# Low parts of the first layer's weights by TensorE and ACT instead of POOL, in a kernel of attention, a Fourier mix and a two-layer network

## The chip, the cores and the metric

The kernel runs on one core of one Trainium2 chip. The metric is the device time of one execution in microseconds (us). Five engines work side by side, each through its own list of instructions in order: TensorE (PE; its weight loads are shown as PEld), VectorE (DVE), ACT, POOL and SP, which here only issues transfers. Matrix products go to PSUM, in banks of 128 x 512 float32 numbers; everything else lies in SBUF.

## The reference

```python
def _attn_ref(q, k, v):                        # 8 batches, 8 heads, 576 positions, 64 wide
    scores = scale * np.matmul(q, k.transpose(0, 1, 3, 2))
    scores = np.where(block_i >= block_j, scores, -1e9)      # blocks of 64
    attn = np.exp(scores - np.max(scores, axis=-1, keepdims=True))
    attn = attn / (np.sum(attn, axis=-1, keepdims=True) + 1e-09)
    return np.matmul(attn, v)

def _moe_ref(x, w_ch1, w_ch2):                 # x: 8 x 576 x 512, weights 512 x 2048 and 2048 x 512
    X = np.fft.fft(np.fft.fft(x, axis=1), axis=2)
    u = x + np.real(X)
    un = (u - mean(u)) / np.sqrt(var(u) + 1e-06)
    return u + np.maximum(un @ w_ch1, 0.0) @ w_ch2
```

`x` is the output of the attention with the heads side by side. The weights are float64, all else is float32.

## The kernel before, in words

To keep the accuracy of float32 with float16 products, the kernel splits each operand in a high part, rounded to float16, and a low part, the rest, also float16. A product is then three products: high by high, high by low, low by high. This is done for the weights (`W`, with index 0 the high and 1 the low part), for the normalized rows (`uh`, `ul`), the hidden layer (`gh`, `gl`, later kept in tiles that are named `zc`, `zs` and `fs` after earlier users), the probabilities (`ph`, `pl`) and V (`VH`, `VL`).

The work goes batch by batch. For each head there are four products for the row maxima (tile `M`), four for the scores, and the values (`av`, 45 products). When the eight heads of a batch are done, a Fourier transform by products with constant tables follows (`dft`): rows are gathered (`U`, `X`, `u`), folded on VectorE (`tmp`, `fs`), multiplied in two stages (`fs` to `zc` and `zs`, these to `bs`, `dif` and `add`), and POOL adds the results to `u`. Then 256 rows at a time are normalized (`st`, `ag`, `un`), transposed (`uh`, `ul`) and given as a "feed" to the two layers: `h` is the first layer's result, `acc` the second's. A feed has 192 first-layer and 96 second-layer products and fills gaps that the heads leave.

The weights are prepared during the first batch and a half. A load brings two tiles of 128 x 512 (the last four loads one each) as 64-bit words. "Unpacking" (`weight_single`) makes float32 numbers of their bits with one `TENSOR_SCALAR` and two `SCALAR_TENSOR_TENSOR` on VectorE (rows `W<-W` or, for the last four, `W<-u`), then ACT sums their squares (`left`). When a layer's sixteen tiles are unpacked, `weight_scale` makes a power of two out of the sum (`wst`), and `weight_parts` splits each tile: for the second layer by ACT and VectorE, for the first by ACT (high part, and a scaled copy in a scratch tile named `p32`, shown as `p`) and POOL (copy less high part). Raw tile `i` lies where parts `i + 2` will lie, so the parts follow each other in order.

The order of all instructions is set by a planner at build time. Each piece of work is a `Step` with a cost on TensorE, a chain of costs on other engines (D VectorE, A ACT, G POOL, X VectorE and the shared queue K, p the two scratch tiles, B a PSUM bank coming free), the steps that it comes after, and keys that must be done. The planner books queues with these costs and takes from several lanes what is ready; steps of the second batch's heads wait until the first layer's weights are done (`("w", 15)`). The lists of the engines are fixed by it, so a changed cost moves other work too. Almost every instruction is recorded by a helper, so in the profile PE's line is 217 and the other engines' is 195.

Of the kernel before, what the change touches and what calls it, by code (L numbers as in the profile page):

```python
# [9 lines left out]
F32 = mybir.dt.float32  # L10
F32R = mybir.dt.float32r
F16 = mybir.dt.float16
I32 = mybir.dt.int32
AF = mybir.ActivationFunctionType
ALU = mybir.AluOpType
# [4 lines left out]
B, H, S, D = 8, 8, 576, 64  # L20
DM = H * D
FF = 4 * DM
P = 128
NF = FF // P
# [177 lines left out]
def tile_attn_fourier_ffn(  # L202
# [5 lines left out]
    work = pool("work")  # L208
# [4 lines left out]
    def ps_tile():  # L213
        return ps[current].tile([P, 512], F32, name=current)

    def mm(*args, **kw):
        return tc.keep_in_program_order(nc.tensor.matmul(*args, **kw))  # L217
# [4 lines left out]
    vector, scalar, gpsimd, sync = (Ordered(tc, x) for x in (nc.vector, nc.scalar, nc.gpsimd, nc.sync))  # L222
# [4 lines left out]
    ident = ident_r.bitcast(F32)  # L227
# [24 lines left out]
    X1, X0, QA, QB = [], [], [], []  # L252
# [23 lines left out]
    for at in range(0, NCOS, P):  # L276
        w = min(P, NCOS - at)
        vector.tensor_scalar(ZT[:, at:at + w], ones[:, 0:w], 0.0, None, op0=ALU.mult)

    W = const.tile([P, 2 * NF + 2, 2, DM], F16, name="W")  # L280
# [14 lines left out]
    def may(step):  # L295
        return all(x in done for x in step.after) and all(x in done for x in step.need)

    def ready(step):
        r = max((done[x] for x in step.after), default=0.0)
        return max(r, min(rings[x][0] for x in lent)) if step.bank else r  # L300
# [780 lines left out]
    wst = work.tile([P, 8], F32, name="wst")  # L1081
# [28 lines left out]
    def weight_single(x):  # L1110
        i, n, at = LANDS[x]
        r = raw(x).rearrange("p (n x) -> p x n", x=2)
        t = W[:, i + 2:i + 2 + n].rearrange("p i x n -> p (i x n)").bitcast(I32)
        vector.tensor_scalar(t, r[:, 1], 3, 0x3FFFFFFF, op0=ALU.logical_shift_left, op1=ALU.bitwise_and)
        yield
        vector.scalar_tensor_tensor(t, r[:, 0], 29, t, op0=ALU.logical_shift_right, op1=ALU.bitwise_or)
        yield
        vector.scalar_tensor_tensor(t, r[:, 1], -(1 << 30), t, op0=ALU.bitwise_and, op1=ALU.bitwise_or)
        yield
        scalar.activation(wjunk[:, 0:DM * n], t.bitcast(F32), AF.Square, accum_out=wsum[:, i:i + 1])  # L1120
        if n == 2:
            gpsimd.memset(wsum[:, i + 1:i + 2], 0.0)
        yield

    def weight_sum(w):
        vector.tensor_reduce(wst[:, 4 * w:4 * w + 1], wsum[:, NF * w:NF * (w + 1)], axis=AX.X, op=ALU.add)
        yield

    def weight_scale(w):

        n2, sc, inv = (wst[:, 4 * w + i:4 * w + i + 1] for i in range(3))
        t = ps_tile()
        mm(t[:, 0:1], ones, n2, start=True, stop=True)
        yield
        vector.tensor_copy(n2, t[:, 0:1])
        e = (10, 14)[w]
        x = work.tile([P, 1], I32, name="pw", bufs=2)
        vector.tensor_scalar(x, n2.bitcast(I32), 0x7F000000, 1, op0=ALU.bitwise_and, op1=ALU.logical_shift_right)
        vector.tensor_scalar(sc.bitcast(I32), x, -1, (190 + e) << 23, op0=ALU.mult, op1=ALU.add)
        vector.tensor_scalar(inv.bitcast(I32), x, (64 - e) << 23, None, op0=ALU.add)  # L1140
        if w == 1:
            vector.tensor_tensor(inv_w, wst[:, 2:3], wst[:, 6:7], op=ALU.mult)
        yield

    def weight_parts(i):
        t = W[:, i + 2].rearrange("p x n -> p (x n)").bitcast(F32)
        w = i // NF
        sc = wst[:, 4 * w + 1:4 * w + 2]
        scalar.activation(W[:, i, 0], t, AF.Copy, scale=sc)
        yield  # L1150
        if w == 0:
            scaled = work.tile([P, 512], F32, name="p32", bufs=2)
            scalar.activation(scaled, t, AF.Copy, scale=sc)
            yield
            gpsimd.tensor_tensor(W[:, i, 1], scaled, W[:, i, 0], op=ALU.subtract)
            yield
            return
        vector.scalar_tensor_tensor(W[:, i, 1], t, sc, W[:, i, 0], op0=ALU.mult, op1=ALU.subtract)
        yield

# [10 lines left out]
    def weight_lane(w):  # L1171

        for x, (i, n, at) in enumerate(LANDS):
            if i // NF == w:
                yield Step(
                    lambda: weight_single(x), 0.0, (f"D{0.19 + 0.53 * n}", f"D{0.19 + 0.51 * n}", f"D{0.19 + 0.51 * n}", f"A{0.38 + 0.43 * n}"),
                    (("WL", x),) + ((("WS", x - 1),) if x else ()) + ((("scale", 0), ('V', 7, 4)) if w else ()), ("WS", x),
                )
        if w == 1:
            yield Step(lambda: None, 0.0, (), (), "w32")  # L1180
        yield Step(lambda: weight_sum(w), 0.0, ("D0.16",), tuple(("WS", x) for x, y in enumerate(LANDS) if y[0] // NF == w), ("sum", w))
        yield Step(lambda: weight_scale(w), 0.1, ("B", "D0.45"), (("sum", w),), ("scale", w), True)
        for j in range(NF):
            yield Step(
                lambda: weight_parts(NF * w + j), 0.0, ("A0.73", "X0.75") if w else ("A0.73", "p1", "A0.72", "G1.2", "p"), (("scale", w),) + ((("w", NF * w + j - 2),) if NF * w + j > 1 else ()), ("w", NF * w + j),
            )

    def store(b, c):
# [25 lines left out]
    lanes = [table_lane(), head_lane(), prepare_lane(), pair_lane(), copy_lane(), v_lane(), max_lane(), score_lane(), value_lane(), transform_lane()]  # L1214
    heads = [next(x) for x in lanes]
    weights, filler = [load_lane(), *(weight_lane(w) for w in range(2))], None
    sides = [next(x) for x in weights]
    while True:
# [23 lines left out]
        else:  # L1242
            w = None
# [5 lines left out]
        if soon:  # L1249
            i = min(soon, key=lambda i: heads[i].place)  # L1250
        elif feed and ready(filler) <= now or feed and not able:
            i = None
        elif able:
            i = min(able, key=lambda i: ready(heads[i]))
        elif any(sides):
            w = min((w for w, x in enumerate(sides) if x is not None and may(x)), key=lambda w: ready(sides[w]))
# [62 lines left out]
```

## Time and profile before

| | |
|---|---|
| runs (us) | 1246.78, 1252.19, 1253.78; median 1252.19 |
| profiled execution (us) | 1252.79, span 1251.0 |
| mean granted TensorE clock | 0.937 |
| busy: PE, PEld, DVE, ACT, POOL | 92%, 66%, 57%, 45%, 35% |

In the rows of the profile, "x3" counts the instructions of a row and `out<-in` names tiles. Rows by time give the start, the time from the first start to the last end of the row, the engine and the operation, and in brackets how long the engine was idle before and what ended that. Rows by stage give, for each stretch of time, its length, then the busy time of PE, PEld, DVE, ACT and POOL with counts, the granted TensorE clock, and the share and rate of the transfers. Rows by group give busy time and mean ns, then the idle time before them; rows by tile give the shortest, median and longest duration in ns and the first and last start.

### The profile page before, as it was taken

The numbers are of one execution on the slowest core, as the hardware profiler recorded it, in microseconds if no ns is written. First come the engines' busy times: TensorE is split into PE (matmuls) and PEld (weight loads), VectorE is DVE, ScalarE is ACT, GpSimd is POOL, SyncE is SP. The second block draws the span as 40 slices with busy tenths as digits, with TensorE's granted clock in tenths as the row PEclk, the third lists the DMA queues.
The fourth block names the chain that finished last, engine by engine and source line by source line (L and its number), as shares of the span: only waits on it lengthen the run. The fifth ranks groups of instructions, "written<-read, shape, count | busy, mean of one in ns | idle before, by whom it ended". The sixth has DMA issues, their size and how long they took to land.

```text
span 1251.0 us, 25235 instructions
## 1 busy us (share of the span) xinstructions
PE 1145.8 (92%) x10068; PEld 829.5 (66%) x10068; DVE 709.6 (57%) x1520; ACT 562.3 (45%) x1249; POOL 433.4 (35%) x522
## 2 busy tenths in 40 slices
PE   5773387999799999999999999999999999999998
PEld 4662374577577777776667767776777667766665
DVE  6878778776656664756647665576545324421211
ACT  5555656755464554644555445554542112111110
POOL 4654732433443633353343533335342200300000
PEclk9655776999799999999999999999999999999999
DMA  7684334361334232431335232422230110000000
GB/s 208 194 266 139 106 103 126 78 176 41 97 93 124 53 106 75 114 109 52 88 87 153 73 86 69 123 73 85 69 84 15 37 37 1 22 18 1 18 18 17
DMA packets 65099, 107.38 MB, mean 86 GB/s; under 512 B 9504, under 2 KB 35304, under 8 KB 64982
## 3 DMA queue, kind: packets, MB, share of 16 engines
q1 hardware_dynamic: 57606, 81.37, 23.5%
q10 hardware_dynamic: 4384, 16.78, 4.0%
q0 software_dynamic: 2992, 7.62, 2.2%
q8 instruction: 79, 1.29, 0.5%
q14 instruction: 38, 0.31, 0.1%
HBM read 58.54 MB, written 18.89 MB: 62 GB/s over the span
## 4 chain that ended last, share of the span: by engine, by line
PE 79%; DVE 10%; POOL 3%; DMA 3%; issue 2%; ACT 2%; SPq 0%; DVEq 0%; ACTq 0%; POOLq 0%
PE acc L217 30%; PE h L217 29%; PE ps L217 14%; PE av L217 6%; DVE W L195 3%; DVE M L195 2%; DMA lead<-mt 1%; PE ps L220 1%; POOL u L195 1%; DVE VL L195 1%; DVE rest L195 1%; DMA U<-xd,rows 1%; POOL pl L195 1%; SPq L195 0%; POOL ag L195 0%
## 5 line engine op out<-in xcount | busy, mean ns | idle before, releaser
L217 PE MATMUL h<-uh,W 128*128 128x256 f16 x2304 | 427.6, 273 | 2.0 <-DVE gl L195 1.2
L195 POOL TENSOR_TENSOR pl<-p,ph 128x288 f16<-128x288 f32 (+1 forms) x256 | 255.2, 1012 | 410.5 <-ACT p L195 395.2
L217 PEld LDWEIGHTS <-W 128*128 128x128 f16 x3456 | 332.1, 98 | 65.0 <-issue 3.7
L217 PE MATMUL acc<-W,gh 128*128 128x512 f16 x1104 | 330.4, 381 | 1.1 <-DVE W L195 1.0
L217 PE MATMUL h<-ul,W 128*128 128x256 f16 x1152 | 314.5, 273 | 0.3 <-issue 0.3
L195 ACT ACTIVATE gh<-h 128x512 f16<-128x512 f32 x138 | 82.4, 598 | 295.5 <-PE h L217 295.3
L217 PE MATMUL acc<-W,gl 128*128 128x512 f16 x552 | 209.6, 380 | 1.3 <-DVE gl L195 1.3
L195 DVE SCALAR_TENSOR_TENSOR gl<-h,gh 128x512 f16<-128x512 f32 x138 | 94.6, 688 | 204.2 <-ACT gh L195 204.1
L195 DVE TENSOR_REDUCE M<-ps 128x1 fp32r<-128x320 f32 (+3 forms) x293 | 132.1, 487 | 127.1 <-PE ps L217 126.7
L217 PE MATMUL ps<-lead 73*128 73x288 f16 (+13 forms) x694 | 165.4, 300 | 17.1 <-DMA lead<-in_c_masks_dram 7.0
L195 ACT ACTIVATE ph<-ps 128x288 f16<-128x288 f32 (+1 forms) x231 | 116.4, 506 | 98.7 <-PE ps L217 97.9
L217 PEld LDWEIGHTS <-gh 128*128 128x128 f16 x1104 | 102.5, 99 | 83.9 <-issue 3.8
L217 PEld LDWEIGHTS <-ph 128*128 128x128 f16 x1920 | 116.9, 105 | 23.1 <-issue 2.6
L217 PE MATMUL av<-VH,pl 128*128 128x65 f16 x960 | 119.0, 203 | 7.0 <-POOL pl L195 6.8
L217 PE MATMUL av<-VH,ph 128*128 128x65 f16 x960 | 120.2, 205 | 1.5 <-DVE zc L195 1.5
L217 PE MATMUL av<-VL,ph 128*128 128x64 f16 x960 | 119.4, 202 | 0.0
L195 ACT ACTIVATE p<-ps 128x288 f32<-128x288 f32 (+1 forms) x231 | 116.6, 507 | 2.7 <-POOL pl L195 2.7
L217 PE MATMUL ps<-rest 128*128 128x320 f16 (+3 forms) x344 | 97.6, 296 | 7.2 <-DVE M L195 6.2
L217 PEld LDWEIGHTS <-pl 128*128 128x128 f16 x960 | 95.7, 104 | 9.1 <-POOL pl L195 8.8
L217 PEld LDWEIGHTS <-gl 128*128 128x128 f16 x552 | 53.9, 98 | 70.1 <-DVE gl L195 3.3
L217 PEld LDWEIGHTS <-lead 73*128 73x128 f16 (+1 forms) x672 | 58.2, 101 | 62.6 <-issue 20.8
L217 PEld LDWEIGHTS <-rest 128*128 128x128 f16 x336 | 34.0, 101 | 21.8 <-issue 3.5
(186 smaller groups left out, 1427.0 us busy)
## 6 DMA issues: line engine op xcount, KB each, us to landing
raw<-in_qk_dram SPq DMA_DIRECT2D x28, 576.0 KB
W<-in_moe_w_ch_dram ACTq DMA_DIRECT2D x14, 1024.0 KB
rest<-lead SPq DMA_DIRECT2D x72, 144.0 KB
V<-in_v_dram SPq DMA_DIRECT2D x32, 320.0 KB
out_dram<-u SPq DMA_DIRECT2D x32, 256.0 KB
rest<-rest SPq DMA_DIRECT2D x56, 144.0 KB
xd<-x SPq DMA_DIRECT2D x30, 256.0 KB
u<-xd SPq DMA_DIRECT2D x8, 512.0 KB
```

The costliest lines, as they stand in the source:

```text
L195: x = f(*args, **kw)
L217: return tc.keep_in_program_order(nc.tensor.matmul(*args, **kw))
L220: return tc.keep_in_program_order(nc.tensor.transpose(*args, **kw))
```

## The change

The first layer's low parts are no longer made by POOL from a scaled copy. Two tiles are made once: `ident` times minus the scale in float32, and `ident` in float16; both lie in a tile named `x`, which also holds the attention's results on their way out. For each weight tile TensorE then computes, in one PSUM bank, the float32 product of the first with the unpacked tile plus the float16 product of the second with the high part. That is the high part less the scaled weight, and ACT writes it with the opposite sign as the low part. The high part becomes a step of its own (`weight_high`), and the steps have new costs: 1.2 on TensorE, 0.6 on ACT, nothing on POOL, and no scratch tile.

```diff
+    turns = []
+
+    def weight_high(i):
+        t = W[:, i + 2].rearrange("p x n -> p (x n)").bitcast(F32)
+        scalar.activation(W[:, i, 0], t, AF.Copy, scale=wst[:, 1:2])
+        yield
+
     def weight_parts(i):
...
+        if w == 0:
+            if i == 0:
+                both = work.tile([P, 10 * D], F32, name="x", bufs=1)
+                turns.extend((both[:, 0:P], both[:, P:P + P // 2].bitcast(F16)))
+                vector.tensor_scalar(turns[0], ident, sc, -1.0, op0=ALU.mult, op1=ALU.mult)
+                vector.tensor_copy(turns[1], ident)
+                yield
+            left = ps_tile()
+            mm(left, turns[0], t, start=True, stop=False)
+            mm(left, turns[1], W[:, i, 0], start=False, stop=True)
+            yield
+            scalar.activation(W[:, i, 1], left, AF.Copy, scale=-1.0)
+            yield
+            return
         scalar.activation(W[:, i, 0], t, AF.Copy, scale=sc)
         yield
-        if w == 0:
-            scaled = work.tile([P, 512], F32, name="p32", bufs=2)
-            scalar.activation(scaled, t, AF.Copy, scale=sc)
-            yield
-            gpsimd.tensor_tensor(W[:, i, 1], scaled, W[:, i, 0], op=ALU.subtract)
-            yield
-            return
...
+            if w == 0:
+                yield Step(
+                    lambda: weight_high(j), 0.0, ("A0.73",), (("scale", 0),) + ((("w", j - 2),) if j > 1 else ()), ("whigh", j),
+                )
+                yield Step(
+                    lambda: weight_parts(j), 1.2, (("D0.5",) if j == 0 else ()) + ("A0.6",), (("whigh", j),), ("w", j), True,
+                    need=(("V", 5, 4),),
+                )
+                continue
```

The planner's order changes from there to the end. On TensorE, in the first batch's Fourier transform, before (`dft` with `fs` and `uh` is the first stage):

```order
L217 MATMUL h<-ident,M_90 5x128
L217 MATMUL h<-dft,fs_1295 128x290 x3
L217 MATMUL h<-dft,fs_1307 128x290 x3
L217 MATMUL h<-dft,fs_1291 128x290
L217 MATMUL acc<-dft,fs_1295 128x290 x3
```

and after the change, where `W,x` is a product of a weight tile with one of the two new tiles:

```order
L217 MATMUL ps<-W,x 128x512
L217 MATMUL h<-dft,fs_1305 128x290 x3
L217 MATMUL h<-dft,fs_1319 128x290 x3
L217 MATMUL h<-dft,fs_1300 128x290
L217 MATMUL h<-W,x 128x512
L217 LDWEIGHTS x
L217 MATMUL h<-W,x 128x512
L217 MATMUL acc<-dft,fs_1305 128x290 x3
```

Six of the sixteen pairs of products stand ahead of the first stage, seven between the products of the two stages, and three behind them. On ACT, where the splitting begins, before (`lead`, `rest` and `VH` are the high parts of heads 8 and 9):

```order
L195 ACTIVATE W<-W,wst 128x512
L195 ACTIVATE p_1209<-W,wst 128x512
L195 ACTIVATE W<-W,wst 128x512
L195 ACTIVATE p_1215<-W,wst 128x512
L195 ACTIVATE lead_1155<-raw,vacc 128x576
L195 ACTIVATE rest_1156<-raw,vacc 128x576
L195 ACTIVATE VH_94<-V,vacc 128x10x64
```

and after (`W<-acc` and `W<-ps` are low parts out of PSUM):

```order
L195 ACTIVATE W<-W,wst 128x512 x2
L195 ACTIVATE W<-acc 128x512
L195 ACTIVATE lead_1155<-raw,vacc 128x576
L195 ACTIVATE rest_1156<-raw,vacc 128x576
L195 ACTIVATE VH_94<-V,vacc 128x10x64
L195 ACTIVATE W<-ps 128x512
```

The first low part, which waits for TensorE, stands ahead of head 8's high parts. On VectorE, in feed 1's first layer, before (`zc`, `zs` and `fs` are low parts of the hidden layer, the last of them `fs`; `W<-W` and `W<-u` are unpackings, `M_90` belongs to head 10):

```order
L195 SCALAR_TENSOR_TENSOR zc_1910<-h,zc_1910 128x512
L195 SCALAR_TENSOR_TENSOR zc_1922<-h,zc_1922 128x512
L195 TENSOR_SCALAR W<-W 128x1024
L195 SCALAR_TENSOR_TENSOR W<-W 128x1024 x2
L195 SCALAR_TENSOR_TENSOR zs_1957<-h,zs_1957 128x512
L195 TENSOR_REDUCE M_90<-ps 128x2
L195 TENSOR_REDUCE M_90<-ps 128x1 x3
L195 SCALAR_TENSOR_TENSOR zs_2024<-h,zs_2024 128x512
L195 SCALAR_TENSOR_TENSOR fs_2038<-h,fs_2038 128x512
L195 TENSOR_SCALAR W<-u 128x512
```

and after, a little earlier in it:

```order
L195 TENSOR_SCALAR W<-u 128x512
L195 SCALAR_TENSOR_TENSOR W<-u,W 128x512 x2
L195 TENSOR_REDUCE M_90<-ps 128x2
L195 TENSOR_REDUCE M_90<-ps 128x1
L195 TENSOR_SCALAR W<-u 128x512
L195 SCALAR_TENSOR_TENSOR W<-u,W 128x512
L195 TENSOR_REDUCE M_90<-ps 128x1
L195 SCALAR_TENSOR_TENSOR zc_1941<-h,zc_1941 128x512
```

Before, five unpackings are left when the second `ul` of feed 1 is made, and three of them come behind feed 1's first layer. Now four are left, and all four stand within it. The earlier ones have moved too: one more whole unpacking stands ahead of the first fold, and the one that stood right behind the last Fourier sum of the batch stands before that sum.

More of the change, by code (lines that the diff above doesn't have):

```diff
@@ L1183, in weight_lane @@
         for j in range(NF):
+            if w == 0:
[7 more added lines that the diff above has]
+                continue
             yield Step(
-                lambda: weight_parts(NF * w + j), 0.0, ("A0.73", "X0.75") if w else ("A0.73", "p1", "A0.72", "G1.2", "p"), (("scale", w),) + ((("w", NF * w + j - 2),) if NF * w + j > 1 else ()), ("w", NF * w + j),
+                lambda: weight_parts(NF * w + j), 0.0, ("A0.73", "X0.75"), (("scale", w), ("w", NF * w + j - 2)), ("w", NF * w + j),
             )
```

## The prediction

> **What bounds the kernel now.** I read the slices of the page first, then the busy time by stage, then the chain that ended last inside the stage of the change, then the engines' rows there.
>
> ```profile
> PE   5773387999799999999999999999999999999998
> PEclk9655776999799999999999999999999999999999
> ```
>
> From the eighth slice on (one is 31 us) TensorE is full and at its full clock, but for a dip at slice 11. What happens before that counts only by how much TensorE work it leaves undone. The same by stages:
>
> ```profile
> core 0: us, PE busy (x) PEld busy (x) DVE busy (x) ACT busy (x) POOL busy (x), PEclk, DMA share, GB/s
> 96.00:116.00 20.00, 2.42 (x9) 0.97 (x8) 17.77 (x28) 12.68 (x22) 11.84 (x13) 0.50 0.57 184
> 116.00:143.00 27.00, 16.04 (x83) 13.08 (x83) 19.08 (x29) 15.90 (x32) 15.09 (x18) 0.75 0.18 59
> 143.00:165.50 22.50, 10.12 (x75) 6.80 (x76) 21.84 (x34) 12.34 (x30) 14.08 (x20) 0.50 0.24 77
> 190.00:222.00 32.00, 22.63 (x165) 14.47 (x163) 27.67 (x63) 20.12 (x47) 8.08 (x9) 0.68 0.36 109
> 319.00:341.00 22.00, 14.60 (x115) 10.15 (x116) 15.36 (x36) 8.29 (x20) 10.76 (x17) 0.69 0.34 99
> ```
>
> "Loss" below means length less busy time times clock. From 96 to 165.5 us TensorE does 1.2 + 12.0 + 5.1 = 18 us of full-clock work in 69.5 us, a loss of 51. From 190 to 222 it loses 32 - 22.63 x 0.68 = 16.6 and from 319 to 341 it loses 11.9. So there are two places to win: the stage of the change (96 to 165.5), and 190 to 222, where the second layer's weights are late. There VectorE is the busy engine.
>
> In the stage of the change VectorE and POOL hold each other up:
>
> ```profile
> 98.56 0.68 DVE L195 TENSOR_SCALAR W<-W 128x1024 int32<-128x1024 int32 x1
> 100.46 0.85 DVE L195 SCALAR_TENSOR_TENSOR VL<-V,vacc,VH 128x640 f16<-128x640 f32 x1
> 110.86 0.68 DVE L195 TENSOR_TENSOR tmp<-X,U 33x512 f32<-33x512 f32 x1 [1.43 <-DMA U<-xd,rows]
> 113.09 0.42 DVE L195 TENSOR_TENSOR fs<-tmp,fs 32x257 fp32r<-32x257 f32 x1
> 114.42 2.95 DVE L195 TENSOR_TENSOR fs<-tmp,fs 128x257 fp32r<-128x257 f32 x1 [0.46 <-ACT p L195]
> 143.67 5.90 DVE L195 TENSOR_SCALAR W<-W 128x1024 int32<-128x1024 int32 x1
> 181.85 0.68 DVE L195 TENSOR_SCALAR W<-W 128x1024 int32<-128x1024 int32 x1
> 182.57 2.49 DVE L195 SCALAR_TENSOR_TENSOR W<-W 128x1024 int32<-128x1024 int32 x2
> 211.17 0.17 DVE L195 TENSOR_REDUCE wst<-ul 128x1 f32<-128x16 f32 x1 [0.92 <-ACT left L195]
> ```
>
> ```profile
> 114.80 2.27 POOL L195 TENSOR_TENSOR W<-p,W 128x512 f16<-128x512 f32 x2
> 142.89 1.15 POOL L195 TENSOR_TENSOR W<-p,W 128x512 f16<-128x512 f32 x1
> 146.77 2.25 POOL L195 TENSOR_TENSOR W<-p,W 128x512 f16<-128x512 f32 x2
> ```
>
> A VectorE instruction that meets POOL's subtractions lasts until these are over: 2.95 us from 114.42 while two run (a like one took 0.42), 5.90 from 143.67 (the same form took 0.68 at 181.85), until 149.57, with the last subtraction over at 149.02. Both lie on the chain that ended last, and some of the subtractions themselves too (start, us, what):
>
> ```profile
> 114.42 2.95 DVE fs L195
> ...
> 132.86 1.33 POOL W L195
> 134.28 2.02 POOL W L195
> ...
> 139.04 1.14 POOL W L195
> ...
> 143.75 5.84 DVE W L195
> ...
> 165.47 7.50 PE h L217 x51
> ```
>
> Until 110.86 the chain is the gather that VectorE waits for in that row; what POOL holds up ahead of it costs nothing.
>
> **What is removed.** Sixteen subtractions of 1.29 us leave POOL:
>
> ```profile
> L195 POOL TENSOR_TENSOR W<-p,W 128x512 f16<-128x512 f32 x16 | 20.5, 1291 | 13.4 <-ACT p L195 13.1
> ```
>
> POOL's 20.5 us have no worth of their own, only the stalls do, and what of them stands on the chain. At 114.42 it is 2.95 - 0.42 = 2.5 us. Three pieces of the chain are subtractions that stand ahead of the Fourier sums on POOL: 1.33 + 2.02 + 1.14 = 4.5. At 143.67 POOL's own additions on the Fourier sums run in any case, but without the 1.15 ahead of them and the 2.25 behind them the block ends 3.4 us sooner. Sum: 10.4 us off the chain.
>
> **What is added.** ACT reads sixteen low parts of 512 columns from PSUM, a form that takes 0.60, where it wrote sixteen scaled copies of that size: one for one, no charge. VectorE makes the two diagonals once: at most the 0.68 of the 1024 columns at 98.56 for each, rather 0.3, since they have 128. TensorE gets, for each tile, a float32 product of 512 columns and a float16 one. Its rows:
>
> ```profile
> L195 ACT ACTIVATE gh<-h 128x512 f16<-128x512 f32 x138 | 82.4, 598 | 295.5 <-PE h L217 295.3
> L220 PE MATMUL ps<-ident,un x64: 272/273/308, 447.2 to 860.6; 128*128 128x128 f32 x64
> L217 PE MATMUL h<-uh,W x256: 269/273/417, 165.5 to 307.6; 128*128 128x256 f16 x128
> L217 PE MATMUL acc<-W,gh x80: 376/379/393, 217.1 to 317.5; 128*128 128x512 f16 x80
> 213.84 1.92 PE L220 MATMUL ps<-ident,un 128*128 128x128 f32 x8
> ```
>
> A float32 instruction of 128 columns lasts as long as a float16 one of 256 (273), and four transposes are eight records: each float32 product is two passes at half the rate. From 256 to 512 float16 columns is 379 - 273 = 106 ns more, so 512 float32 columns are 2 x 4 x 106 = 0.85 us, the float16 product 0.21, together 1.07 us at full clock (at least 0.64, were it three float16 products). At half clock the eight records took 1.92, 0.24 per 128 columns and pass, so 8 x 0.24 + 0.43 = 2.35 us. I take 1.2 and 2.4 with weight loads. Sixteen are 19 us of TensorE work at full clock, which fits the loss of 51: no charge, unless a tile stands ahead of something on the chain. It does at two places, and the new order adds a third charge.
>
> First, ACT's order now has the first low part ahead of head 8's high parts (`lead`, `rest`) and VH, which were done early:
>
> ```profile
> 97.45 0.78 ACT L195 ACTIVATE lead<-raw,vacc 128x576 f16<-128x576 f32 x1 [0.33 <-DVE vacc L195]
> 99.17 0.82 ACT L195 ACTIVATE VH<-V,vacc 128x640 f16<-128x640 f32 x1
> ```
>
> The diagonals come about 99.2, the first tile ends at 102 (half clock), the low part at 102.6, and with two high parts and VH of some 0.7 to 0.8 each VH ends at 104.8, where VectorE had started on VL at 100.46. VectorE then still has VL, an unpacking, head 8's low parts and maxima (about 6 us unblocked), and one whole unpacking (0.68 + 2.49) that the order moved up to here. So the fold that started at 110.86 starts near 114: +3.1. Second, seven tiles stand between the Fourier stages. The clock, 0.50 in the row from 96 to 116, rises within the stages of before:
>
> ```profile
> 119.00:122.40 3.40, 3.40 (x13) 2.93 (x14) 3.27 (x8) 1.70 (x5) 0.00 (x0) 0.50 0.00 0
> 122.40:125.80 3.40, 3.24 (x17) 2.43 (x15) 2.58 (x6) 1.37 (x4) 0.00 (x0) 0.65 0.00 0
> ```
>
> After 3.4 us at work without a break it begins to rise (0.65 as the mean of the next 3.4 us, so about 5 us in all). So one or two tiles cost 2.4 and the rest 1.2; VectorE's unpackings, now 3.2 each, cover all but the first two: +3.5. The Trainium skill has this rule in "TensorE: Matmul & The Clock Gate", Part 1: about 3.4 us of sustained work lifts the gate, about as long an idle stretch drops it again. By it the tiles from 99 us on would themselves have lifted the clock, and the second charge would be 2.4 instead of 3.5; the rows above agree that work alone lifts it, after a little longer.
>
> Third, unpackings move ahead. The one at 143.67 now stands before the last Fourier sum. There it still waits for POOL's additions and then adds 0.68 + 2.49 = 3.2; behind the sum it no longer costs the rest of its 5.90 (2.5) and its two further passes (2.5): -1.8. The one of 181.85 takes the place ahead of the second `ul` that the one before it had, so its own time costs nothing; for its load, which is asked for later than that one's, and POOL's work beside it I take +1.5 (0 to 4). Together `ul`, on which feed 1 waits, moves by -10.4 + 3.1 + 3.5 - 1.8 + 1.5 = -4.1. Feed 1, at 165.47 before, starts some 5.8 earlier, for head 9's scores no longer stand ahead of it; these cost 1.3 at full clock later. So the first term is **-4.5** (bounds: +9 if all seven tiles cost 2.4 on the path, 16.8 instead of 3.5; -12 if none of the charges falls on it, 10.4 + 1.8).
>
> **The second term** is 190 to 222. The unpacking of 181.85 would end near 156, and the four last ones, and the sum at 211.17 that all second-layer weights wait for, follow in the order one by one within feed 1's first layer instead of behind it. TensorE then has second-layer products to fill the 16.6 us of loss. VectorE does the same work as before, so I take half of it: **-8.5** (bounds 0 and -16.6).
>
> Sum: -13 on a profiled time of 1252.8 (span 1251.0; the median of runs is 1252.2): **1240 us**. What hides TensorE's 19 us is idle time; what may be late next is head 15, which ends the dip at 319 to 341.
>
> **Rivals.** *All of the second loss comes back*: -4.5 - 16.6, 1232. For it: the order has second-layer products before head 10's end, where it had none. Against: VectorE was at 27.67 of 32 there. *Nothing reaches the end*: the lead of the first layers is spent waiting at 319 to 341, where TensorE hangs on the next batch's heads and not on weights; the 11.9 us lost there would grow by the 13 won, 1253. *Slower*: TensorE stays at half clock, because ACT and TensorE now wait for each other (a high part waits for the product two tiles earlier, in a buffer that both read), and each of the seven tiles puts 2.4 us between Fourier stages that follow one another directly. Then the first term is its upper bound, +9, and with none of the second term the time is 1262. It decides, with the second term, from 2.4 us per tile on the chain (7 x 2.4 is about 3.5 + 13), without it from 1.1 (3.5 + 4.5). Against it is the clock's rise at 122.4. *The change doesn't do what it says* is no rival: the order has no subtraction on POOL left.
>
> **Chances.** Forecast (1235 to 1246) 0.43; second loss wholly back (below 1235) 0.20; nothing reaches the end (1246 to 1258) 0.21; slower (above 1258) 0.16. A change of 0.5%, 6.3 us, is about what a measurement of this kernel can tell from none. So faster 0.63, same 0.21, slower 0.16. The range 1228 to 1260 leaves out the last part of both outer cases.
>
> **What would show it.** Right: the `fs` row at 0.4 instead of 2.95, no VectorE row of 5.9, feed 1 near 160, the sum of second-layer squares near 190 instead of 211, TensorE losing about 8 between there and 222. Wrong: the fold starts well after 114 (ACT behind the first tile costs more), the granted clock stays 0.50 past 125, tiles of over 2 us stand on the chain, or the dip after 319 grows.

## The result and the profile after

The changed kernel is faster: median 1235.82 us (1232.19 to 1236.84, four runs) against 1252.99 of the kernel before beside it, ratio 0.9866 with a 95% interval from 0.9825 to 0.9907. The profiled execution took 1235.12, span 1233.3, mean granted clock 0.959. A second set of six runs of the same kernel, told below, gave 0.9915 (0.9898 to 0.9933). So the gain is some 11 to 17 us, and the forecast of 13 lies between.

The stages that the prediction used, and 251 to 319, to which the dip moved:

```profile
96.00:116.00 20.00, 13.56 (x24) 4.94 (x25) 14.02 (x25) 11.09 (x21) 3.69 (x6) 0.67 0.66 219
116.00:143.00 27.00, 23.70 (x102) 15.02 (x102) 21.46 (x35) 19.38 (x40) 10.09 (x15) 0.88 0.16 48
143.00:165.50 22.50, 12.16 (x107) 8.70 (x107) 19.07 (x39) 13.64 (x31) 10.25 (x16) 0.70 0.48 152
190.00:222.00 32.00, 27.00 (x266) 16.21 (x267) 25.12 (x53) 25.66 (x57) 12.67 (x13) 1.00 0.42 109
251.00:319.00 68.00, 61.66 (x549) 44.16 (x548) 51.09 (x110) 35.96 (x83) 31.58 (x39) 0.92 0.37 106
319.00:341.00 22.00, 21.97 (x234) 17.07 (x233) 13.04 (x33) 12.07 (x29) 8.46 (x11) 1.00 0.21 53
```

From 190 to 222 TensorE loses 5.0 us (32 - 27.00 x 1.00) where it lost 16.6. The dip that lay at 319 to 341 lies ahead of 319 now and costs 68 - 61.66 x 0.92 = 11.3, about the 11.9 of before: it moved with the work and did not grow. In the stage of the change (engine rows by time):

```profile
108.00 2.34 PE L217 MATMUL acc<-W,x 128*128 128x512 f32 x3
112.55 0.67 DVE L195 TENSOR_TENSOR tmp<-X,U 33x512 f32<-33x512 f32 x1
115.86 0.43 DVE L195 TENSOR_TENSOR fs<-tmp,fs 128x257 fp32r<-128x257 f32 x1
123.58 1.24 PE L217 MATMUL ps<-W,x 128*128 128x512 f32 x3
136.43 1.11 DVE L195 TENSOR_SCALAR W<-W 128x1024 int32<-128x1024 int32 x1
156.04 0.68 DVE L195 TENSOR_TENSOR ul<-acc,uh 128x512 f16<-128x512 f32 x1
160.15 0.21 DVE L195 TENSOR_SCALAR M<-M 128x1 fp32r<-128x1 f32 x1
160.42 0.27 PE L217 MATMUL h<-ident,M 128*5 128x128 f32 x1 [7.61 <-DVE M L195]
160.49 0.44 PE L217 MATMUL h<-uh,W 128*128 128x256 f16 x1
188.94 0.16 DVE L195 TENSOR_REDUCE wst<-ul 128x1 f32<-128x16 f32 x1
```

The `fs` row lasts 0.43 instead of 2.95, the unpacking that lasted 5.90 lasts 1.11, feed 1 starts at 160.49 instead of 165.47, and the second layer's squares are summed at 188.94 instead of 211.17. A tile's products last 1.24 or 2.34 us, by the clock.

One thing here is not in the prediction. Feed 1's first product does not wait for the second `ul`, which is written from 156.04 to 156.72. It stands on TensorE right behind the transposition of head 9's row maxima (`h<-ident,M`), and that product waits for VectorE's last row `M<-M`, which ends at 160.36; TensorE is idle for 7.61 us ahead of it. In the kernel before this transposition runs at 157.35, long before feed 1, which starts 2.5 us after the start of the second `ul` (162.95) there.

### The profile page after: what moved, and what is told of

Same layout as the page of the kernel before. It is cut to its first block, busy times and chain, and to the rows that moved or that the text cites. A ratio compares the mean times of both kernels' runs of the same rounds, so it can differ in the third digit from the quotient of the medians.

```text
span 1233.3 us, 25293 instructions
## 1 busy us (share of the span) xinstructions
PE 1151.2 (93%) x10116; PEld 826.7 (67%) x10116; DVE 696.2 (56%) x1522; ACT 561.1 (45%) x1249; POOL 413.8 (34%) x506
## 4 chain that ended last, share of the span: by engine, by line
PE 80%; DVE 10%; DMA 4%; POOL 2%; ACT 2%; issue 2%; SPq 0%; DVEq 0%; ACTq 0%; POOLq 0%
PE acc L217 30%; PE h L217 28%; PE ps L217 15%; PE av L217 6%; DVE W L195 3%; DVE M L195 2%; DMA lead<-rest 2%; DMA lead<-mt 1%; PE ps L220 1%; POOL u L195 1%; POOL pl L195 1%; DVE tmp L195 1%; POOL ag L195 1%; DVE rest L195 1%; DMA lead<-in_c_masks_dram 0%
## 5 line engine op out<-in xcount | busy, mean ns | idle before, releaser
L217 PE MATMUL ps<-lead 72*128 72x64 f16 (+13 forms) x702 | 161.4, 292 | 20.1 <-DMA lead<-in_c_masks_dram 7.1
L195 ACT ACTIVATE ph<-ps 128x512 f16<-128x512 f32 (+1 forms) x234 | 118.5, 508 | 111.7 <-PE ps L217 110.8
L217 PEld LDWEIGHTS <-ph 128*128 128x128 f16 x1920 | 112.4, 103 | 23.1 <-issue 2.8
L195 ACT ACTIVATE p<-ps 128x512 f32<-128x512 f32 (+1 forms) x234 | 118.6, 508 | 5.9 <-POOL pl L195 5.7
L217 PE MATMUL av<-VH,pl 128*128 128x65 f16 x960 | 114.5, 200 | 7.0 <-POOL pl L195 5.1
L217 PE MATMUL av<-VH,ph 128*128 128x65 f16 x960 | 115.8, 201 | 1.5 <-DVE zc L195 1.5
L217 PE MATMUL av<-VL,ph 128*128 128x64 f16 x960 | 115.1, 199 | 0.0
L217 PE MATMUL ps<-rest 128*128 128x320 f16 (+2 forms) x350 | 97.0, 292 | 6.3 <-DVE M L195 4.7
L217 PEld LDWEIGHTS <-pl 128*128 128x128 f16 x960 | 93.2, 102 | 8.7 <-POOL pl L195 6.9
L217 PEld LDWEIGHTS <-lead 72*128 72x128 f16 (+1 forms) x672 | 57.5, 99 | 46.0 <-issue 11.8
```

Source lines behind the costliest of these rows:

```text
L195: x = f(*args, **kw)
```

## The experiments

"High" is the first high part of the weights (`W<-W,wst` on ACT), with which the splitting begins, "feed 1" the first product `h<-uh,W` of feed 1, "sum" the second layer's sum of squares, all three from the one profile of each kernel; ratios are to the kernel before in the same set, with 95% intervals. "Old" and "new" are the orders of the kernels before and after.

| kernel | order | low parts | high | feed 1 | sum | ratio |
|---|---|---|---|---|---|---|
| before | old | POOL | 94.52 | 165.47 | 211.17 | 1 |
| e1 | old | none | 93.20 | 154.03 | 199.34 | 0.9924 (0.9903-0.9944) |
| e6 | old | TensorE | 93.83 | 158.81 | 205.34 | 0.9963 (0.9950-0.9976) |
| e2 | new | POOL | 92.78 | 170.10 | 198.48 | 0.9977 (0.9964-0.9989) |
| after | new | TensorE | 92.88 | 160.49 | 188.94 | 0.9866 (0.9825-0.9907) |
| e5, after again | new | TensorE | 92.47 | 159.94 | 188.13 | 0.9915 (0.9898-0.9933) |
| e7, as after up to 650 us | new | TensorE | 93.97 | 160.19 | 189.83 | 0.9925 (0.9904-0.9946) |
| e3 | new | float16 product only | 92.68 | 159.40 | 188.03 | 0.9892 (0.9870-0.9915) |
| e8, as e3 up to 650 us | new | float16 product only | 94.05 | 161.10 | 192.36 | 0.9905 (0.9885-0.9925) |
| e4 | new | float32 product twice | 94.33 | 162.77 | 192.40 | 0.9919 (0.9901-0.9938) |

e5 is the kernel after in a second profile, e7 differs from it only behind 650 us, and e8 only there from e3. So one program starts the splitting up to 1.5 us earlier or later and reaches feed 1 up to 1.7 us apart (e3, e8). Differences of that size between single profiles show nothing. Part of it stands ahead of the change, where TensorE's clock from 65 to 70 us is full in the kernel after and half in e7:

```profile
65.00:70.00 5.00, 3.52 (x61) 3.21 (x59) 3.70 (x12) 2.87 (x8) 4.21 (x4) 1.00 0.76 250
```

```profile
65.00:70.00 5.00, 4.71 (x34) 4.37 (x34) 2.67 (x8) 2.44 (x5) 3.90 (x4) 0.50 0.78 240
```

**e1, the stalls alone.** The kernel before, without POOL's part:

```diff
-            scaled = work.tile([P, 512], F32, name="p32", bufs=2)
-            scalar.activation(scaled, t, AF.Copy, scale=sc)
+            scalar.activation(W[:, i, 1], t, AF.Copy, scale=sc)
             yield
-            gpsimd.tensor_tensor(W[:, i, 1], scaled, W[:, i, 0], op=ALU.subtract)
```

> The kernel before with its order, but POOL makes no low part: ACT's second pass over each tile writes another high part where the low part would be (the subtraction is left out, so the first layer's weights are wrong). Nothing is added on TensorE. Theory A (the gain is POOL's stalls taken off the chain up to feed 1, and then second-layer weights that are ready in time): the fs row is 0.4 us instead of 2.95, the 5.90 us row is 0.7, feed 1 starts 8 to 11 us before 165.5, and about as much reaches the end, since the order of the late unpackings is that of before and the loss ahead of the second layer stays near 16: 1242 to 1245 us. Theory B (the gain comes from the new order alone, whatever POOL does): no more than 2 us, 1250 to 1253.

1243.80 us (1239.58 to 1245.32). Rows of VectorE and TensorE, and the stage in which it loses time ahead of the second layer:

```profile
113.29 0.43 DVE L195 TENSOR_TENSOR fs<-tmp,fs 128x257 fp32r<-128x257 f32 x1 [0.46 <-ACT W L195]
136.55 1.07 DVE L195 TENSOR_SCALAR W<-W 128x1024 int32<-128x1024 int32 x1
154.03 0.37 PE L217 MATMUL h<-uh,W 128*128 128x256 f16 x1 [0.81 <-ACT p L195]
...
178.00:210.00 32.00, 22.76 (x166) 14.51 (x165) 27.67 (x63) 20.09 (x47) 7.89 (x9) 0.68 0.35 102
```

Both stalls are gone, feed 1 starts 11.4 us earlier (8 to 11 were expected; 1.3 of the 11.4 stand already at the first high part, where both kernels have run the same instructions), and the loss ahead of the second layer is untouched: 32 - 22.76 x 0.68 = 16.5, the same stretch 12 us earlier. Theory B, that POOL's work is of no account, falls.

**e2, the order alone.** The kernel after, with POOL again:

```diff
...
-            left = ps_tile()
-            mm(left, turns[0], t, start=True, stop=False)
-            mm(left, turns[1], W[:, i, 0], start=False, stop=True)
+            ps_tile()
             yield
-            scalar.activation(W[:, i, 1], left, AF.Copy, scale=-1.0)
+            scaled = work.tile([P, 512], F32, name="p32", bufs=2)
+            scalar.activation(scaled, t, AF.Copy, scale=sc)
+            gpsimd.tensor_tensor(W[:, i, 1], scaled, W[:, i, 0], op=ALU.subtract)
```

> The order of the kernel after on all engines, but the low parts are made as before: ACT writes the scaled copy at the place of its low part, POOL subtracts, and TensorE has neither of the two products. Theory A: VectorE's rows beside POOL are long again and the Fourier sums wait for subtractions, so of the 10.4 us most comes back, less the 3.5 that the tiles between the Fourier stages cost: feed 1 at 163 to 168 instead of 160.4, the time 1239 to 1245. Theory B (order alone): the time of the kernel after, 1234 to 1238. Theory C (TensorE's added products pay by lifting its clock ahead of the Fourier stages): the granted clock between 96 and 116 us falls back to 0.50 and the Fourier stages last longer, 1240 or more, with the stall rows short.

1250.66 us (1247.84 to 1252.05), above theory A's range, at feed 1 too (163 to 168 were expected), and far above B's. C's "1240 or more" holds it, and the clock is 0.50 from 96 to 116 us as C has it, but not with short stall rows: the first unpacking behind the fold takes 1.45 us instead of 0.70, and on POOL the subtractions stand among the Fourier sums again, in the new order later than in the old, and feed 1 with them:

```profile
142.87 1.69 POOL L195 TENSOR_TENSOR W<-p,W 128x512 f16<-128x512 f32 x1 [1.98 <-ACT p L195]
144.53 1.71 POOL L195 TENSOR_TENSOR u<-u,dif 128x257 f32<-128x257 f32 x1
...
148.25 1.15 POOL L195 TENSOR_TENSOR W<-p,W 128x512 f16<-128x512 f32 x1
...
170.10 0.44 PE L217 MATMUL h<-uh,W 128*128 128x256 f16 x1
...
190.00:222.00 32.00, 28.66 (x273) 19.46 (x271) 27.86 (x60) 24.17 (x53) 8.38 (x8) 1.00 0.38 99
```

The second loss shrinks to 3.3 although POOL still makes the low parts: the second term belongs to the order. It is not only that feed 1 comes later within this stretch. The sum comes 28 us behind feed 1 in e2 and in the kernel after, and 45 to 47 behind it in the three kernels of the old order. But feed 1 starts 4.6 us later than in before, and of all this 2.9 us (0.23%, by the ratio) are left at the end. The order pays only without the stalls.

**e6, the engines alone.** The old order, with TensorE's products at the place of the scaled copies (the body of `weight_parts` from the kernel after, the steps of before):

```diff
-            scaled = work.tile([P, 512], F32, name="p32", bufs=2)
-            scalar.activation(scaled, t, AF.Copy, scale=sc)
-            yield
-            gpsimd.tensor_tensor(W[:, i, 1], scaled, W[:, i, 0], op=ALU.subtract)
...
+            left = ps["acc"].tile([P, 512], F32, name="acc")
+            mm(left, turns[0], t, start=True, stop=False)
+            mm(left, turns[1], W[:, i, 0], start=False, stop=True)
+            scalar.activation(W[:, i, 1], left, AF.Copy, scale=-1.0)
+            yield
             yield
```

> The order of the kernel before on all engines; each low part is made by TensorE's two products and ACT's read of PSUM, at the place where ACT wrote the scaled copy, and POOL has nothing of it. Theory A (stalls off the chain up to feed 1; the second term comes from the order): feed 1 starts 1 to 6 us after the 154.0 of the kernel of that order without low parts, the sum of the second layer's squares comes some 45 us behind it as in before, and the time is 1243 to 1248. Theory B (what counts is that TensorE makes them, wherever): the time of the kernel after, 1234 to 1238.

1248.41 us (1247.20 to 1249.30), a hair above theory A's range and far from B's.

```profile
112.17 0.67 DVE L195 TENSOR_TENSOR tmp<-X,U 33x512 f32<-33x512 f32 x1
158.81 0.37 PE L217 MATMUL h<-uh,W 128*128 128x256 f16 x1 [0.84 <-ACT p L195]
...
190.00:222.00 32.00, 23.92 (x193) 14.34 (x193) 27.18 (x57) 22.36 (x53) 12.04 (x12) 0.79 0.40 111
```

In the old order the products cost 4.8 us of feed 1's start (158.81 against e1's 154.03), 2.4 of it ahead of the fold (112.17 against 109.73 there), and the second loss is 13.1. Against before this is 4.6 us faster by the ratio; against the kernel after in the same set (1241.37) it is 7.0 slower by the medians. e1, which does none of the new work, is no faster than the kernel after, which does all of it: what the new order wins at least pays for the products.

**e3 and e4, less and more of TensorE's work.** The float32 product left out, and done twice:

```diff
 e3
-            mm(left, turns[0], t, start=True, stop=False)
-            mm(left, turns[1], W[:, i, 0], start=False, stop=True)
+            mm(left, turns[1], W[:, i, 0], start=True, stop=True)
 e4
             mm(left, turns[0], t, start=True, stop=False)
+            mm(left, turns[0], t, start=False, stop=False)
             mm(left, turns[1], W[:, i, 0], start=False, stop=True)
```

> The kernel after without the float32 product of each tile; the float16 product, ACT's read of PSUM and all waits stay (the low parts are wrong). Theory A (the tiles cost only where they stand ahead of the chain): feed 1 starts 2 to 4 us before 160.4 and the time is 1231 to 1234. Theory C (the products pay by the clock): the granted clock is 0.50 through 116 to 125 us, feed 1 is not earlier, and the time is 1236 to 1242. If all 16 us of products were on the path it would be 1222.

> The kernel after with the float32 product of each tile done twice into the same bank (the low parts are wrong): 14 us more of TensorE at full clock, 27 at half. Theory A: of sixteen tiles the first costs 1.7 us ahead of head 8's high parts and seven cost 0.85 to 1.7 between the Fourier stages, where VectorE's unpackings cover part: feed 1 4 to 8 us later, the time 1239 to 1244. If TensorE's work is free, 1234 to 1238; if all of it is on the path, 1250.

e3: 1239.41 us (1236.52 to 1241.91); e4: 1243.12 (1240.32 to 1244.18). The stage from 96 to 116 us of e3, then of e4:

```profile
96.00:116.00 20.00, 5.20 (x15) 2.13 (x16) 14.69 (x25) 11.32 (x21) 5.54 (x9) 0.50 0.66 217
```

```profile
96.00:116.00 20.00, 16.24 (x36) 6.87 (x37) 14.68 (x30) 10.63 (x20) 3.12 (x5) 0.76 0.72 225
```

The float32 products do lift the clock (0.50, 0.67, 0.76 for none, one, two). By these profiles feed 1 starts 1.1 us later with one than with none, which the spread between e3 and e8 (159.40, 161.10) swallows, and 2.3 later again with two, of which 1.5 stand already at the first high part. So e4 came within its range by the time, but not by feed 1 (4 to 8 us were expected). e3's time is that of theory C, and not below that of the kernel after; feed 1 moved by less than the 2 to 4 of theory A. Where e3 and the kernel after part shows at head 46's transfers (`lead<-rest`), in the kernel after and in e3:

```profile
653.32 0.30 PE L217 MATMUL ps<-lead 72*128 72x64 f16 x3 [1.57 <-DMA lead<-rest]
```

```profile
655.09 0.42 PE L217 MATMUL ps<-lead 72*128 72x64 f16 x3 [3.48 <-DMA lead<-rest]
...
655.00:660.00 5.00, 4.91 (x28) 2.58 (x29) 3.33 (x8) 0.00 (x0) 0.00 (x0) 0.50 0.27 65
```

Until 648 both run alike within 0.2 us. The same transfer then takes 5.04 us in one execution and 6.75 in the other; the longer wait is followed by half clock.

**e5, e7, e8: is that wait the difference?** The kernel after again, and both kernels with work for TensorE ahead of head 46 (`max_part`):

```diff
+        if (h, n) == (46, 0):
+            for _ in range(7):
+                mm(t, W[:, 0, 0, 0:P], W[:, 0, 0], start=True, stop=True)
```

> The kernel after, unchanged, beside the others of this set, with a second profiled execution. If its lead over the kernel without the float32 product (1235.8 to 1239.4) is a matter of one wait that falls now short, now long (head 46's transfers at 653 us: 1.6 us of waiting at full clock in the first profile of the kernel after, 3.5 us and then half clock in that of the other), the new profile may show either, and the median lies at 1234 to 1239. If the lead is of the kernel itself, the wait is 1.6 us again and the median 1234 to 1237.

> The kernel after with seven float16 products of 512 columns (1.5 us at full clock, results overwritten) ahead of head 46's first product for the maxima, which waits 1.6 us or more for its transfers at 653 us. If a wait of about 3 us costs 3 us more by the clock that falls behind it, the wait's idle part stays under 2.2 us, the clock stays at 1.00 there, and the time is 1233 to 1236, with a narrower spread than the kernel after beside it. If the clock has nothing to do with it, the time is that of the kernel after or up to 1.5 us more.

> The kernel without the float32 product (wrong low parts), with the same seven products ahead of head 46. If its 3.6 us behind the kernel after come from the long wait and the half clock at 653 us, they go: 1234 to 1237, that is 2.5 to 5 us less than without the seven products. Theory C (the float32 products pay, by the clock that they hold up between 99 and 143 us): it stays at 1238 to 1241.

e5: 1241.37 us (1238.40 to 1245.14), above what was expected either way; e7: 1243.01 (1238.99 to 1247.00); e8: 1242.03 (1237.97 to 1245.03). The wait in e5:

```profile
658.30 0.30 PE L217 MATMUL ps<-lead 72*128 72x64 f16 x3 [2.50 <-DMA lead<-rest]
...
658.30:663.00 4.70, 4.70 (x53) 2.97 (x54) 4.29 (x9) 0.92 (x3) 0.00 (x0) 1.00 0.37 84
```

The wait does vary from execution to execution of one kernel (1.57, 2.50). Filling it works where it stands: behind the seven products e8 waits 1.28 us at 662.06 and keeps the clock at 1.00. But it wins nothing that the times show: my explanation of e3 by this one wait falls. Nor does the clock theory stand: e8 without the float32 product (0.9905) and e7 with it (0.9925) are the same within their intervals, as are e3 and e5. The lead of the kernel after over e3 lies within the spread of its own runs, which go from 1232.19 to 1245.14 over the two sets.

**e9, the dip.** The kernel after, with the two integer instructions of `scale` reading PSUM:

```diff
-        bits, to = n2.bitcast(I32), sc.bitcast(I32)
+        bits, to = t[:, 0:3].bitcast(I32), sc.bitcast(I32)
```

> The kernel after, with the two integer instructions (pw) that make a head pair's scale reading the sums in PSUM instead of their copy in SBUF; nothing else changes. In the kernel after one of them lasts 2.15 us at 300.59, where it takes 0.17 elsewhere, while POOL adds on Fourier results; behind it TensorE waits 2.2, 1.0, 0.6 and 1.3 us, its clock falls to 0.50, and 9.9 us are lost from 300 to 319. Theory D (the stall by POOL starts this dip): the row takes 0.2 to 0.7, TensorE's first wait there falls under 1 us, the loss is 3 to 7, and the time 2 to 6 us under that of the kernel after (0.991 and 0.987 of before in two sets): 0.983 to 0.988 of before. Rival: the next to be late is a transfer (head 20's copies, which the chain shows from 302.30 to 305.25), the loss stays over 8, and the time 0.987 to 0.992.

1234.54 us (1233.62 to 1234.60), ratio 0.9865 (0.9845 to 0.9884): in the range of theory D, but not by its way. The row in the kernel after, then the place in e9 with POOL beside it and the stage:

```profile
300.59 2.15 DVE L195 TENSOR_SCALAR pw<-vacc 128x2 int32<-128x2 int32 x1
```

```profile
302.00 0.15 DVE L195 TENSOR_SCALAR pw<-ps 128x2 int32<-128x2 int32 x1
302.19 2.75 DVE L195 SCALAR_TENSOR_TENSOR vacc<-pw 128x1 int32<-128x1 int32 x2
...
299.91 2.28 POOL L195 TENSOR_TENSOR pl<-p,ph 128x512 f16<-128x512 f32 x2
302.16 0.72 POOL L195 TENSOR_TENSOR u<-u,dif 128x257 f32<-128x257 f32 x1
302.85 1.39 POOL L195 TENSOR_TENSOR u<-u,add 128x255 f32<-128x255 f32 x2
304.21 0.71 POOL L195 TENSOR_TENSOR u<-u,dif 128x255 f32<-128x255 f32 x1
...
300.00:319.00 19.00, 14.06 (x127) 9.88 (x127) 16.48 (x36) 7.00 (x16) 13.38 (x18) 0.64 0.51 144
```

The instruction now takes 0.15 beside POOL's `pl` (299.91 to 302.19), and the next one, which reads SBUF twice, takes over the stall, until POOL's additions end. The loss is 19 - 14.06 x 0.64 = 10.0, no smaller than in the kernel after, and the interval of the ratio overlaps that kernel's: a gain is not shown. The Trainium skill ("SBUF — State Buffer", Who interferes with whom) says that a VectorE instruction with two SBUF inputs contends with POOL and one with at most one outside the two-port modes does not; these rows agree with both halves.

**e10, e11, e12: other orders.** One condition or number of the planner changed:

```diff
 e10, e12 (low parts)
-                    need=(("V", 5, 4),),
+                    need=(("N", 4),),
 e11
-AHEAD = (3.0, 6.0)
+AHEAD = (4.5, 6.0)
 e12
-AHEAD = (3.0, 6.0)
+AHEAD = (2.0, 6.0)
```

> The kernel after with the condition of the low parts' steps changed from head 5's values to V's split for heads 8 and 9, so that the first low part stands behind head 8's high parts and VH on ACT, and six tiles instead of eight between the products of the Fourier stages. If the first tile ahead of the high parts cost what the prediction charged (3.1 us at the fold), the fold starts 1 to 3 us earlier than 112.6 and feed 1 at 157 to 159.5. If what delays the fold is the unpacking on VectorE that the order has ahead of it in both, both stay within 0.8 us of 112.6 and 160.5. The time within 3 us of the kernel after either way, 0.985 to 0.992 of before.

> The kernel after with one number of the planner changed (how far ahead VectorE may be booked for weights, 3.0 to 4.5), which leaves the order as it is up to the second layer's parts at about 215 us and changes it from there to the end. Feed 1 and the sum of squares stay at 160.5 and 189. If the time is decided by then, it is that of the kernel after, 0.987 to 0.992 of before. If the order of the later heads decides a good part, its loss from 222 us to the end differs from the 24 to 27 us of the kernel after by 4 us or more, and the time with it: 0.980 to 0.984 or over 0.995.

> The kernel after with the low parts' steps bound to V's split for heads 8 and 9 and the planner's number for VectorE at 2.0 instead of 3.0. The order then runs the Fourier stages without a weight tile among them; six of the sixteen tiles' pairs of products stand ahead of feed 1's first product and ten inside its first layer. Theory A (the pairs are nearly free only because they lie in time that TensorE would idle): the tiles inside feed 1 cost their 1.1 us each, 11 us in all, the unpackings come later too, and the time is 1243 to 1252 although the Fourier stages end earlier than in the kernel after. If TensorE has time for them anywhere, or the shorter way to feed 1 pays more, it is under 1238.

e10: 1237.30 us (1237.07 to 1239.52), 0.9891 (0.9873 to 0.9908). e11: 1235.43 (1230.99 to 1240.59), 0.9880 (0.9854 to 0.9906). e12: 1261.78 (1260.43 to 1264.10), 1.0078 (1.0058 to 1.0098). The fold and feed 1 in e10:

```profile
108.39 0.68 DVE L195 TENSOR_TENSOR tmp<-X,U 33x512 f32<-33x512 f32 x1 [1.01 <-DMA U<-xd,rows]
158.68 0.44 PE L217 MATMUL h<-uh,W 128*128 128x256 f16 x1
```

So the first low part ahead of head 8's high parts did cost the fold 4.2 us (1 to 3 were expected), but at most 1.8 of these reach feed 1, and the time shows none. e11 keeps the first 215 us and changes all behind; its time stays in the range of the kernel after, as it would if the gain were decided by then. e12 starts feed 1 earliest of all and is the slowest:

```profile
138.55 0.27 PE L217 MATMUL h<-uh,W 128*128 128x256 f16 x1
189.51 0.17 DVE L195 TENSOR_REDUCE wst<-ul 128x1 f32<-128x16 f32 x1 [0.45 <-ACT left L195]
...
165.00:200.00 35.00, 25.50 (x215) 17.53 (x215) 26.56 (x67) 27.66 (x67) 9.38 (x10) 0.76 0.40 116
222.00:900.00 678.00, 647.65 (x6293) 469.22 (x6292) 420.68 (x974) 353.76 (x822) 273.53 (x326) 0.97 0.34 92
```

The time lies above my range, and the 11 us of products inside feed 1 are not enough to explain it. It ran feed 1 out before the heads were under way: 15.6 us are lost from 165 to 200 behind it, and about 50 from 222 to 900, where the kernel after loses about 23. That the late heads are the cause I read from the order and these stretches; no run takes them away by themselves.

## Why the prediction was right

The time (1235.82, and 1241.37 in the other set) lies around the 1240 forecast. Both causes are shown by experiments that separate them: e1 takes the stalls away in the old order, and e2 has the new order with the stalls. The sum also owes something to luck, since several of its parts were off in opposite directions.

- **The stalls, 10.4 us off the chain.** e1 gives 11.4 at feed 1, or 10.1 counted from the first high part. Right.
- **The charge of +3.1 ahead of the fold.** Against e1's fold at 109.73, which waits for the gather, the kernel after folds at 112.55: 2.8, and e10 shows the cause that was named. e2, with no product on TensorE, still folds at 111.51, so most of it is the order on ACT and VectorE and not the product itself.
- **The charge of +3.5 between the Fourier stages.** Too large for the float32 products: with and without them feed 1 differs by no more than executions of one program do. The unpackings that I took to cover all but two tiles seem to cover nearly all. e3 keeps the float16 product and the waits between ACT and TensorE, so these are not measured alone. The rise of the clock, which I put at about 5 us of work, also comes out later from the same two rows: a mean of 0.65 over 3.4 us is 2.4 us at half clock, so 5.8 in all.
- **The moved unpackings, -1.8 and +1.5, and what feed 1 waits for.** From the fold to the start of the second `ul` it is 41.8 us in e1 and 43.5 in the kernel after, 1.7 more, where the charge and these two terms together gave 3.2. So the second `ul` came early: 6.9 us before that of the kernel before, where I had 4.1. But the step "`ul`, on which feed 1 waits" does not hold in the new order. Head 9's scores no longer stand ahead of feed 1, as I said, but the transposition of its maxima does, and VectorE ends these 3.6 us after `ul`. Feed 1 therefore moved by 5.0 and not by 5.8.
- **The first term, -4.5.** e6 is 4.6 us faster than before, but with other parts than I added up: its order has none of the moved unpackings. TensorE's account in the kernel after gives less. From 96 to 165.5 it loses 31 us where it lost 51, and the sixteen tiles take up 17 to 20 of the difference (16 x 1.07 to 1.24), so at most 3 us are won in that stage.
- **The second term, -8.5, half of 16.6.** The loss from 190 to 222 fell to 5.0, so 11.6 came back there, more than I took. The sum at 188.94 was forecast near 190. At the end the order is worth 7.0 us (e5 against e6).
- **Rivals.** "Nothing reaches the end" fails: the dip kept its size. "Slower" fails: the clock is 0.88 in the Fourier stages. "All of the second loss" (1232) lies at the lower edge of the first set, but 5.0 of the 16.6 are still lost.

The two terms are not independent, which the prediction did not say: the new order with POOL's stalls (e2) is worth 2.9 us, the stalls' removal in the old order (e6) 4.6, both together 10.7 to 17. Why the times of one kernel scatter is open: within one set by 8.0 us in the kernel before (1249.44 to 1257.49), by 9.6 in e11, by 2.1 in e6 and by 1.0 in e9. The one wait that I could name does not settle it.

## What to carry to other kernels

When an engine's work is moved away because it blocks another, count the blocked rows on the chain and not the busy time that is moved: 20.5 us of POOL were worth 10 to 11 us at feed 1. The new work cost up to 4.8 there in the old order; in the new, where it lay in time that TensorE idled, its float32 products cost no more than executions of one program differ. A changed cost in a planner changes the order, so try engine and order apart: here neither alone gave half of the whole. Engines work their lists in order, so ask of each product not only what it needs but what stands ahead of it: feed 1 had its data at 156.7 and started at 160.5, behind another head's product. Whether moving that product wins these 3.8 us was not tried. An earlier start of one stage need not be a gain: the kernel with the earliest feed 1 (e12) was the slowest, as far as its stages tell because the work that must run beside it came later.

## What the runs showed of the hardware

- The length of one wait does not decide whether the clock falls. At head 46's transfers it stayed at 1.00 behind waits of 1.57 and 2.50 us, and fell behind 3.48 (0.50 in the next 5 us). e10 has 2.91 there, and the 8.4 us behind it at a mean of 0.80:

```profile
653.59 0.30 PE L217 MATMUL ps<-lead 72*128 72x64 f16 x3 [2.91 <-DMA lead<-rest]
...
653.60:662.00 8.40, 8.40 (x72) 5.49 (x73) 7.04 (x15) 2.12 (x6) 1.10 (x2) 0.80 0.54 138
```

  But e11 has a longer wait, 3.33, and keeps full clock, while in the kernel after the clock falls behind waits of 2.21 and 1.00 with one product between them:

```profile
660.76 0.28 PE L217 MATMUL ps<-lead 73*128 73x288 f16 x1 [3.33 <-DMA lead<-mt]
...
661.00:666.00 5.00, 5.00 (x53) 3.70 (x51) 0.72 (x2) 4.77 (x13) 2.63 (x4) 1.00 0.00 0
```

```profile
304.51 0.35 PE L217 MATMUL ps<-lead 72*128 72x448 f16 x1 [2.21 <-DVE add L195]
...
304.00:320.00 16.00, 11.89 (x92) 8.16 (x92) 12.85 (x30) 7.14 (x16) 9.77 (x15) 0.68 0.37 98
```

  The Trainium skill ("TensorE: Matmul & The Clock Gate", HAM oscillation) puts the idle stretch at about 3.4 us; here 2.91 was enough once and 3.33 was not. The time at half clock, worked back from these means (twice the length times what the mean lacks to 1), is 3.4 us in e10 and 10.2 in the kernel after, three times as long.
- A VectorE instruction that meets POOL can wait for a whole run of POOL's instructions, not only for one: 2.75 us in e9 for two instructions, over four additions of 0.7. It goes the other way too: in the kernel after POOL's additions beside an unpacking take 2.85 for two, where they take 1.41 with no unpacking beside them.

```profile
136.94 2.85 POOL L195 TENSOR_TENSOR u<-u,add 128x255 f32<-128x255 f32 x2
...
142.69 1.41 POOL L195 TENSOR_TENSOR u<-u,add 128x255 f32<-128x255 f32 x2
```
